# Moving the left-over scores, the left-over value products and one transposed block of x inside the head-pair loop

## The chip, the cores and the metric

The kernel runs on one core of one Trainium2 chip. The metric is the device time of one execution in microseconds (us). The core's engines are TensorE (PE, with its weight loads shown as PEld), VectorE (DVE), ScalarE (ACT), GpSimd (POOL) and SyncE (SP); each works through its own instructions in order, and semaphores tie them together.

## The reference, cut to what matters

Two layers follow one another: causal attention with a cumulative bias, and a mixing of 64 Fourier modes with a channel product behind it.

```
# q, k, v: (8, 8, 576, 64); s: (8, 8, 576)
scores = q @ k^T / 8;  bias = -(cumsum(max(s,0))[t] - cumsum(max(s,0))[t'])
attn   = softmax(causal(scores + min(bias, 0)))
x      = (attn @ v) with the heads side by side            # (8, 576, 512)
X      = rfft(x, axis=1)[:, :64]                           # 64 modes
Y      = X * (w_r + i w_i), one 512 x 512 matrix per mode  # 2 x 64 matrices from HBM
u      = x + irfft(Y)
out    = u + max(u @ w_ch, 0)
```

All that must be read once is q, k, v and the mode matrices; the latter, 64 x 2 of 512 x 512 in float32, are by far the most.

## The kernel before

**The loop.** N = 32 groups n = 0..31 each hold one pair of heads of one batch: `g, b = divmod(n, 8)`, with four head pairs g and eight batches b. For each group PE makes the scores of both heads (`scores`, h = 0 and 1, in two halves c = 0, 1 of the keys), ACT takes their exponentials into `p_sb`, and PE multiplies them with v (`av`), one group or half a group later. The 576 keys are two windows of 288; 128 + 128 of a window's keys go through the two halves c, and the 32 keys left over in each window go, for both heads together, through `scores4` (lines 368 to 391) into `p4`.

**Order within a group** (lines 586 to 621). This order is written by hand and is each engine's program order: `scores(n, 0)`, `av(n-1, 1)`, `mode_products(n)` where the group has any, `transposes(n+1, 0)`, `scores(n, 1)` with `scores4(n)` in front of its second half, `first_transposed(i, 0)`, `transposes(n+1, 1)`, `fft(n-1)`, `av(n, 0)`, on odd n `place_v(n+1)`, then `first_product(i, 0)`, `first_transposed(i, 1)`, `first_product(i, 1)`. The three steps with i exist in the last six groups (n = 26 to 31) alone: they multiply two token blocks of x, already finished, with w_ch ahead of time. Groups 8, 16 and 24 have another order (lines 595 to 603).

**What the steps do on the engines.** `transposes` (348) turns 18 blocks of q and k on PE into `tr_ps`; for half 0 DVE copies both q and k out (`qt`, `kt`), for half 1 DVE copies q and ACT copies k. `fft` (456) multiplies x of the last group with the Fourier matrix into `ft_ps`, and DVE casts it out in four pieces (line 474). `modes` (476) multiplies the modes with their weight tiles, 16 matmuls for one c of eight, in four steps of four that each need another weight tile; its sum goes to `y_acc` on DVE (502, 504), or for the last g to `y_sb` (508). `first_transposed` (550) makes four transposing matmuls into `xt_ps`, and DVE casts them to `xt1`. `first_product` (561) makes four matmuls into `z1_ps` (`z_ps` in the profile), and ACT copies the sum away (545).

**Accumulator memory.** The pools turn over buffers in the order in which they are asked for. `scpool` has two (scores, left-over scores, placed v), `trpool` one, `avpool` one, `auxpool` two (`yp`, `ft_ps`, `xt_ps`, `z1_ps`). Whoever asks takes the buffer asked for two requests ago (one in `trpool` and `avpool`), and waits until its readers are done.

**Loads.** POOL issues all large loads, in one fixed order (lines 243 to 272, 589): q and k for two groups, v for two groups, and 128 weight tiles of the modes (two transfers of 256 KB each as written), spread between them. A load waits for a free buffer (weights in rings of 11 and 6) and for its lane. SP issues the bias rows (346), small spreads of rows (519) and the stores.

**After the loop** (lines 864 to 967) come the modes of the last g, c = 0 to 7, with the remaining products of x and w_ch between them, and then the inverse transform, the ReLU, the sums and the stores, in a written order. The last weight tiles are used by c = 7 in line 899, whose fourth step follows `first_u`.

Of the kernel before, what the change touches and what calls it, by code (L numbers as in the profile page):

```python
# [18 lines left out]
def kernel(  # L19
# [15 lines left out]
    P = 128  # L35
# [7 lines left out]
    NCH = D + 1  # L43
# [89 lines left out]
    v4 = [ap_.tile([P, 2, 2, VW], FP16, name=f"v4_{i}") for i in range(2)]  # L133
# [6 lines left out]
    p4 = [ap_.tile([P, SP], FP16, name=f"p4_{i}") for i in range(2)]  # L140
# [207 lines left out]
    def transposes(n, half):  # L348
        if n >= N:
            return  # L350
        src = loaded[n][:, n % 2, :].rearrange("p (r d) -> p r d", d=D)[:, half * RH : half * RH + RH]
        ps = trpool.tile([P, RH, 2 * RP], BF16, name="tr_ps", tag="tr")
        for r in range(RH):
            for i in range(2):
                rows = slice(HP * i, HP * i + HP)
                nc.tensor.transpose(ps[rows, r, :], src[rows, r, :], ident16[rows, rows])  # L356
        for i, dst in enumerate((qt, kt)):
            copy = (nc.vector.tensor_copy, nc.scalar.copy)[half * i]
            to, rows = dst[n % NQ][:D], ps[HP * i : HP * i + HP]
            if i == 0:  # L360
                to = to.rearrange("d h (p r) -> d h p r", r=R)[:, :, :, half * RH : half * RH + RH]
                rows = rows.rearrange("d r (h p) -> d h p r", h=2)
            else:
                to = to.rearrange("d h (w r p x) -> d (h w) r p x", w=NWN, r=RV, x=2)[..., half]
                rows = rows.rearrange("d r (i p) -> d i r p", i=2 * NWN)
            copy(out=to, in_=rows)  # L366

    def scores4(n):

        g, b = divmod(n, B)  # L370
        ps = scpool.tile([P, 1024], FP32, name="sc_ps", tag="sc")
        cols = [ps[:, 512 * w : 512 * w + W] for w in range(NWN)]
        for w in range(NWN):
            nc.tensor.matmul(
                cols[w], ident16, negm[:, 2 * W + w * W : 2 * W + (w + 1) * W],
                start=True, stop=False, skip_group_check=True,
            )
        for wq_ in range(NWN):
            for wk in range(wq_ + 1):
                for h in range(2):  # L380
                    r0 = HP * h + RP * wk
                    nc.tensor.matmul(
                        cols[wq_][r0 : r0 + RP], kt[n % NQ][:, h, wk * W + 2 * P : (wk + 1) * W],
                        qt[n % NQ][:, h, wq_ * W : (wq_ + 1) * W],
                        start=False, stop=True, tile_position=(0, r0), skip_group_check=True,
                    )
        nc.scalar.activation(
            out=p4[n % 2][:, :S].rearrange("p (w t) -> p w t", w=NWN),
            in_=ps.rearrange("p (w t) -> p w t", w=NWN)[:, :, :W], func=ACTF.Exp,
            bias=cumt4[:, b * (H // 2) + g : b * (H // 2) + g + 1], scale=0.125,  # L390
        )

    def scores(n, h):
        g, b = divmod(n, B)
        pidx = b * H + 2 * g + h
        qh = qt[n % NQ][:, h, :]
        pt = p_sb[(2 * n + h) % NP_]
        for c in range(2):
            if h == 1 and c == 1:
                scores4(n)  # L400
            ps = scpool.tile([P, 1024], FP32, name="sc_ps", tag="sc")

            for w in range(NWN):
                nc.tensor.matmul(  # L404
                    ps[:, bass.ds(w * S, W)], ident16, negm[:, bass.ts(c, W)],
                    start=True, stop=False, skip_group_check=True,
                )
            for w, i0, i1 in ((0, 0, 512), (0, 512, S), (1, W, S)):
                c0 = w * S + i0 - w * W
                nc.tensor.matmul(  # L410
                    ps[:, c0 : c0 + i1 - i0], kt[n % NQ][:, h, bass.ds(w * W + c * P, P)], qh[:, i0:i1],
                    start=False, stop=True, skip_group_check=True,
                )
            for w in range(NWN):
                x = 2 * w + c
                nc.scalar.activation(  # L416
                    out=pt[:, poff[x] : poff[x] + S - w * W], in_=ps[:, w * S : (w + 1) * S - w * W],
                    func=ACTF.Exp, bias=cumt_sb[:, x, pidx : pidx + 1], scale=0.125,
                )
# [7 lines left out]
    def av(n, h):  # L427
        if n < 0:
            return
        g, b = divmod(n, B)  # L430
        pt = p_sb[(2 * n + h) % NP_]
        ps = avpool.tile([P, NT, VW], FP32, name="av_ps", tag="av")
        todo = []
        for I in range(NT):
            t0 = first_token(b, I)
            for x in range(2 * min((t0 + P - 1) // W + 1, NWN)):
                w, c = divmod(x, 2)
                o = poff[x] + t0 - w * W
                todo.append((I, pt[:, o : o + P], v2[n // 2 % 2][:, NWN * h + w, n % 2, c, :NCH]))
            todo.append((I, p4[n % 2][:, t0 : t0 + P], v4[n // 2 % 2][:, h, n % 2, :NCH]))  # L440

        for i, (I, lhsT, rhs) in enumerate(todo):
            nc.tensor.matmul(  # L443
                ps[:, I, :NCH], lhsT, rhs, start=(i == 0), stop=(i == len(todo) - 1),
                skip_group_check=True,
            )
        rcp = rpool.tile([P, NT], FP32, name="rcp", tag="rcp")
        nc.vector.reciprocal(out=rcp, in_=ps[:, :, D])  # L448
        nc.vector.tensor_tensor(  # L449
            out=x_all[:, g, b, :, D * h : D * h + D],  # L450
            in0=ps[:, :, :D],
            in1=rcp.unsqueeze(2).to_broadcast([P, NT, D]),
            op=ALU.mult,
        )
# [95 lines left out]
    def first_transposed(i, x):  # L550
        b, T = pairs[i][x]
        ps = auxpool.tile([P, DT, P], FP32, name="xt_ps", tag="aux")
        for dt in range(DT):
            nc.tensor.matmul(
                ps[:, dt, :], x_all[:, dt, b, T, :], ident16h, start=True, stop=True,
                skip_group_check=True,
            )
        xts1[i, x] = spool.tile([P, DT, P], FP16, name="xt1", tag="yt")
        nc.vector.tensor_copy(out=xts1[i, x], in_=ps)
# [13 lines left out]
    def mode_products(n, half=None):  # L573
        cs = mode_steps.get(n, [])
        for c in cs if half is None else cs[2 * half : 2 * half + 2]:
            modes(c // NCK, c % NCK)

    with tc.tile_pool(name="sc_psum", bufs=2, space=PSUM) as scpool, \
            tc.tile_pool(name="tr_psum", bufs=1, space=PSUM) as trpool, \
            tc.tile_pool(name="av_psum", bufs=1, space=PSUM) as avpool:  # L580
        cum_rows(0)
        transposes(0, 0)
        transposes(0, 1)
        load(loads_qk(2) + loads_v(2))
        pad_p()
        for n in range(N):
            if n in (0, 2):
                nc.vector.memset(xs_flat[n // 2].bitcast(FP32), 0.0)
            load(loads_qk(n + LA) + loads_v(n + LA) if n % 2 else [], loads_w(on_chip[n]))
            if n == N // 2 + 1:  # L590
                nc.gpsimd.dma_start(out=wch_sb, in_=moe_w_ch.rearrange("(dt p) e -> p dt e", p=P))
            cum_rows(n + 1)
            scores(n, 0)
            av(n - 1, 1)
            if n and n % B == 0:
                scores(n, 1)
                fft(n - 1)
                av(n, 0)
                mode_products(n, 0)
                transposes(n + 1, 0)  # L600
                mode_products(n, 1)
                transposes(n + 1, 1)
                continue
            mode_products(n)
            transposes(n + 1, 0)
            scores(n, 1)
            i = first_pairs[n - N + len(first_pairs)] if n >= N - len(first_pairs) else None
            if i is not None:
                first_transposed(i, 0)
            transposes(n + 1, 1)  # L610
            if n == 0:
                place_v(0)
            fft(n - 1)
            av(n, 0)
            if n % 2:
                place_v(n + 1)
            if i is not None:
                first_product(i, 0)
                first_transposed(i, 1)
            if i is not None:  # L620
                first_product(i, 1)
        av(N - 1, 1)
        fft(N - 1)
# [374 lines left out]
```

## Time and profile before

| | |
|---|---|
| median of 3 runs | 445.63 us (445.6 to 445.71) |
| profiled execution | 445.48 us, span of the profile 443.7 us |
| mean granted TensorE clock | 0.95 |
| PE busy | 351.0 us, 79% |
| ACT, DVE, POOL busy | 258.2, 249.7, 201.8 us |
| DMA | 93.64 MB moved, mean 211 GB/s over the span |

The page and the trace give times from the start of the span. The span leaves out 1.8 us of the execution around it. Busy shares are averages over stages: the loop ends at about 341 us, the modes of the last g run to about 407 us, and the rest finishes and stores the result. A row of a timeline has start, duration, engine, line, operation, output and inputs, count, and in brackets the idle time before it and what ended it. A row of the chain of waits has start, duration and what the time was spent on.

### The profile page before, as it was taken

What the parts mean: (1) busy time and instruction counts of PE and PEld (TensorE: products, weight loads), DVE (VectorE), ACT (ScalarE), POOL (GpSimd) and SP (SyncE); (2) the same over time, 40 slices, a digit from 0 to 9 for tenths busy, and PEclk for the clock granted to TensorE, in tenths of its full rate; (3) what the DMA queues carried; (4) which work ended last, traced back from release to release, by engine and by line L of the source; (5) the groups of instructions that cost most, each with busy time, mean ns of one, the idle gap of its engine ahead of it and who ended that gap; (6) DMA issues with size and microseconds to landing.
All of it is one profiled execution on the core that took longest, in us unless ns stands there. A gap on an engine that the chain in (4) does not pass through costs nothing.

```text
span 443.7 us, 12029 instructions
## 1 busy us (share of the span) xinstructions
PE 351.0 (79%) x5021; PEld 215.5 (49%) x5081; DVE 249.7 (56%) x539; ACT 258.2 (58%) x453; POOL 201.8 (45%) x326
## 2 busy tenths in 40 slices
PE   1578888888898877886957777888887997779992
PEld 1256565555665645654535344555553555433340
DVE  7747566456665654663543534555645554462893
ACT  1388888727877836774655355666662354320992
POOL 5454444443544444444444444444454444420591
PEclk9999999989999998999797988999999799998997
DMA  8999999999999999999999999999999999992696
GB/s 184 213 210 209 209 210 209 209 211 209 209 210 208 209 210 209 208 209 210 209 210 209 210 209 204 209 209 210 210 209 210 209 208 210 204 215 65 231 390 244
DMA packets 55510, 93.64 MB, mean 211 GB/s; under 512 B 8400, under 2 KB 14032, under 8 KB 55456
## 3 DMA queue, kind: packets, MB, share of 16 engines
q0 software_dynamic: 46144, 81.28, 98.9%
q1 hardware_dynamic: 9312, 11.58, 7.9%
q8 instruction: 40, 0.66, 0.5%
q14 instruction: 14, 0.11, 0.1%
HBM read 163.81 MB, written 9.44 MB: 390 GB/s over the span
## 4 chain that ended last, share of the span: by engine, by line
PE 53%; DMA 16%; ACT 14%; DVE 11%; issue 3%; DVEq 0%; ACTq 0%
DMA w_sb<-in_moe_w_r_dram 9%; ACT p_sb L416 9%; PE sc_ps L410 8%; PE sc_ps L404 7%; PE yp L484 6%; PE av_ps L443 6%; PE z_ps L679 5%; DMA w_sb<-in_moe_w_i_dram 4%; PE tr_ps L356 4%; PE ft_ps L464 2%; ACT v L197 2%; DMA qk<-in_k_dram 2%; ACT kt L366 2%; PE z_ps L567 2%; PE u_ps L805 2%
## 5 line engine op out<-in xcount | busy, mean ns | idle before, releaser
L416 ACT ACTIVATE p_sb<-sc_ps,cumt_sb 128x576 f16<-128x576 f32 (+1 forms) x256 | 142.0, 621 | 69.2 <-PE sc_ps L410 68.2
L247 POOL DMA_DIRECT2D w_sb<-in_moe_w_i_dram x120 | 71.0, 592 | 82.7 <-DMA w_sb<-in_moe_w_i_dram 29.5
L247 POOL DMA_DIRECT2D w_sb<-in_moe_w_r_dram x120 | 71.2, 594 | 78.0 <-DMA w_sb<-in_moe_w_r_dram 27.6
L404 PE MATMUL sc_ps<-negm,ident 128*128 128x288 bf16 x256 | 55.0, 298 | 25.2 <-ACT p_sb L416 19.2
L366 DVE COPY qt<-tr_ps 64x576 bf16<-64x576 bf16 x64 | 47.8, 746 | 47.3 <-PE tr_ps L356 47.3
L410 PE MATMUL sc_ps<-qt,kt 128*128 128x64 bf16 (+2 forms) x324 | 58.4, 281 | 10.2 <-ACT kt L366 5.8
L410 PEld LDWEIGHTS <-kt 128*128 128x128 bf16 x384 | 37.9, 101 | 34.2 <-ACT kt L366 10.5
L443 PE MATMUL av_ps<-v,p_sb 128*128 128x65 f16 x1024 | 51.7, 196 | 1.7 <-ACT v L197 1.7
L443 PEld LDWEIGHTS <-p_sb 128*128 128x128 f16 x1024 | 46.1, 98 | 6.3 <-issue 1.9
L443 PE MATMUL av_ps<-v,p 128*128 128x65 f16 x320 | 48.7, 194 | 0.0
L366 ACT COPY kt<-tr_ps 64x576 bf16<-64x576 bf16 x32 | 25.8, 805 | 39.1 <-DVE qt L366 38.5
L356 PE MATMUL tr_ps<-ident,qk 64*64 64x64 bf16 x1152 | 32.4, 201 | 19.5 <-DMA qk<-in_k_dram 9.2
L448 DVE RECIPROCAL rcp<-av_ps 128x5 f32<-128x5 f32 x64 | 12.4, 194 | 59.4 <-PE av_ps L443 58.4
L484 PE MATMUL yp<-w_sb,xs 128*32 128x512 bf16 (+1 forms) x480 | 39.9, 417 | 4.8 <-DMA w_sb<-in_moe_w_i_dram 3.3
L474 DVE CAST xs<-ft_ps 64x128 bf16<-64x128 f32 x128 | 36.7, 287 | 10.1 <-PE ft_ps L464 8.6
L356 PEld LDWEIGHTS <-qk 64*64 64x64 bf16 x1152 | 25.0, 114 | 32.9 <-DVE kt L366 9.7
L404 PEld LDWEIGHTS <-ident 128*128 128x128 bf16 x256 | 20.5, 98 | 41.6 <-issue 38.0
L449 DVE TENSOR_TENSOR x_all<-av_ps,rcp 128x320 f16<-128x320 f32 x64 | 31.5, 492 | 2.2
L443 PEld LDWEIGHTS <-p 128*128 128x128 f16 x320 | 31.6, 100 | 0.0
L484 PEld LDWEIGHTS <-xs 128*32 128x32 bf16 (+1 forms) x512 | 18.2, 145 | 21.2 <-issue 8.1
L366 DVE COPY kt<-tr_ps 64x576 bf16<-64x576 bf16 x32 | 25.6, 801 | 0.4
L545 ACT COPY z<-z_ps 128x512 f32<-128x512 f32 x22 | 12.9, 588 | 19.4 <-PE z_ps L567 11.2
(113 smaller groups left out, 495.0 us busy)
## 6 DMA issues: line engine op xcount, KB each, us to landing
w_sb<-in_moe_w_r_dram POOLq DMA_DIRECT2D x120, 256.0 KB, 9.9
w_sb<-in_moe_w_i_dram POOLq DMA_DIRECT2D x117, 256.0 KB, 9.9
out_dram<-r_w SPq DMA_DIRECT2D x16, 512.0 KB, 3.7
qk<-in_q_dram POOLq DMA_DIRECT2D x15, 288.0 KB, 9.6
qk<-in_k_dram POOLq DMA_DIRECT2D x15, 288.0 KB, 10.1
vf<-in_v_dram POOLq DMA_DIRECT2D x15, 288.0 KB, 10.1
x_all<-in_moe_w_i_dram POOLq DMA_DIRECT2D x6, 256.0 KB, 9.9
y_acc<-in_moe_w_r_dram POOLq DMA_DIRECT2D x4, 256.0 KB, 9.2
```

Of the source, the lines that this page charges most:

```text
L247: nc.gpsimd.dma_start(out=dst, in_=src)
L356: nc.tensor.transpose(ps[rows, r, :], src[rows, r, :], ident16[rows, rows])
L366: copy(out=to, in_=rows)
L404: nc.tensor.matmul(ps[:, bass.ds(w * S, W)], ident16, negm[:, bass.ts(c, W)], start=True, stop=False, skip_group_check=True,)
L410: nc.tensor.matmul(ps[:, c0 : c0 + i1 - i0], kt[n % NQ][:, h, bass.ds(w * W + c * P, P)], qh[:, i0:i1], start=False, stop=True, skip_group ...
L416: nc.scalar.activation(out=pt[:, poff[x] : poff[x] + S - w * W], in_=ps[:, w * S : (w + 1) * S - w * W], func=ACTF.Exp, bias=cumt_sb[:, x, ...
L443: nc.tensor.matmul(ps[:, I, :NCH], lhsT, rhs, start=(i == 0), stop=(i == len(todo) - 1), skip_group_check=True,)
L449: nc.vector.tensor_tensor(out=x_all[:, g, b, :, D * h : D * h + D], in0=ps[:, :, :D], in1=rcp.unsqueeze(2).to_broadcast([P, NT, D]), op=AL ...
L474: nc.vector.tensor_copy(out=xs[g % 2][HP * h : HP * h + HP, q_, :, h, :, b, :], in_=a)
L484: nc.tensor.matmul(ps[32 * cg : 32 * cg + 32, :], cols[k0:, q_, 1 - ri, :, c * MC // 2 + cg], wt[(g, c, ri, cg // 2)][k0:, 2 * (cg % 2) + ...
L545: nc.scalar.copy(out=z1s[i][:, xx], in_=z)
L679: nc.tensor.matmul(zs[i, x], xts[i][:, x, dt, :], wch_sb[:, dt, :], start=(dt == 0), stop=(last and dt == DT - 1), skip_group_check=True,)
```

## The change

Three moves of steps, none added or taken away. `scores4(n)` is called from the loop, between `mode_products(n)` and `transposes(n+1, 0)` (in groups 8, 16 and 24 in front of `scores(n, 1)`), and no more inside `scores(n, 1)`. `first_transposed(i, 1)` stands between `fft(n-1)` and `av(n, 0)`. In `av` the five products with the left-over keys `p4` come after all products with `p_sb`.

```
@@ scores
         for c in range(2):
-            if h == 1 and c == 1:
-                scores4(n)
             ps = scpool.tile([P, 1024], FP32, name="sc_ps", tag="sc")
@@ av
-        todo = []
+        todo, left = [], []
         for I in range(NT):
...
-            todo.append((I, p4[n % 2][:, t0 : t0 + P], v4[n // 2 % 2][:, h, n % 2, :NCH]))
-
+            left.append((I, p4[n % 2][:, t0 : t0 + P], v4[n // 2 % 2][:, h, n % 2, :NCH]))
+
+        todo = todo + left
@@ the loop
             if n and n % B == 0:
+                scores4(n)
                 scores(n, 1)
...
             mode_products(n)
+            scores4(n)
             transposes(n + 1, 0)
             scores(n, 1)
...
             fft(n - 1)
+            if i is not None:
+                first_transposed(i, 1)
             av(n, 0)
             if n % 2:
                 place_v(n + 1)
             if i is not None:
                 first_product(i, 0)
-                first_transposed(i, 1)
-            if i is not None:
                 first_product(i, 1)
```

More of the change, by code (lines that the diff above doesn't have):

```diff
@@ L398, in scores @@
         for c in range(2):
-            if h == 1 and c == 1:
-                scores4(n)
             ps = scpool.tile([P, 1024], FP32, name="sc_ps", tag="sc")
@@ L432, in av @@
         ps = avpool.tile([P, NT, VW], FP32, name="av_ps", tag="av")
-        todo = []
+        todo, left = [], []
         for I in range(NT):
@@ L439, in av @@
                 todo.append((I, pt[:, o : o + P], v2[n // 2 % 2][:, NWN * h + w, n % 2, c, :NCH]))
-            todo.append((I, p4[n % 2][:, t0 : t0 + P], v4[n // 2 % 2][:, h, n % 2, :NCH]))
+            left.append((I, p4[n % 2][:, t0 : t0 + P], v4[n // 2 % 2][:, h, n % 2, :NCH]))
+        todo = todo + left
         for i, (I, lhsT, rhs) in enumerate(todo):
@@ L595 @@
             if n and n % B == 0:
+                scores4(n)
                 scores(n, 1)
@@ L604 @@
             mode_products(n)
+            scores4(n)
             transposes(n + 1, 0)
@@ L613 @@
             fft(n - 1)
+            if i is not None:
+                first_transposed(i, 1)
             av(n, 0)
@@ L618 @@
                 first_product(i, 0)
-                first_transposed(i, 1)
-            if i is not None:
                 first_product(i, 1)
```

## The prediction

> **What bounds the kernel now.** I read the page's DMA row first, then the waits by stage, then the chain and the timeline around the last weights.
>
> ```profile
> DMA  8999999999999999999999999999999999992696
> ...
> q0 software_dynamic: 46144, 81.28, 98.9%
> ```
>
> The DMA engines are full from the start to slice 36 (396 us), at the 209 to 210 GB/s that the windows give. POOL's loads have one order and no spare rate: work done sooner does not make the stream end sooner. Where does the work wait for it? The waits from 200 to 273 us (who waits for whom: us in total, times, longest):
>
> ```profile
> PE tr_ps L356 <- DMA qk<-in_k_dram: 9.2, 2, 5.1
> PE yp L484 <- DMA w_sb<-in_moe_w_i_dram: 3.3, 2, 2.0
> ```
>
> And from 275 to 342 us, the last six groups:
>
> ```profile
> PE z_ps L567 <- DVE xt L559: 5.2, 6, 1.0
> ...
> PE sc_ps L404 <- ACT p_sb L416: 3.5, 6, 0.7
> ```
>
> In the first stretch PE waits for loads, in the second it waits for ACT and DVE alone. The chain changes its nature there:
>
> ```profile
> 262.89 10.00 DMA w_sb<-in_moe_w_i_dram
> 272.94 0.68 PE yp L484 x5
> ```
>
> A weight tile lands at 272.89 us, the middle of group 26 waits for it, and from there the chain is engine work only. So anything saved before 273 us is waited away, and what counts are groups 26 (its second half) to 31. PE has two stalls in each of them; group 28's:
>
> ```profile
> 298.53 0.74 ACT L387 ACTIVATE p<-sc_ps,cumt 128x576 f16<-128x576 f32 x1
> 298.69 0.41 PE L404 MATMUL sc_ps<-negm,ident 128*128 128x288 bf16 x2 [0.68 <-ACT p_sb L416]
> ...
> 303.58 1.04 PE L567 MATMUL z_ps<-wch_sb,xt 128*128 128x512 f16 x4 [0.95 <-DVE xt L559]
> ```
>
> The last half of the scores waits for the score buffer of head 1's first half, and the second product with w_ch waits for the DVE cast of the block just transposed. The end of the stream, by POOL's timeline, by the DMA view of that moment (its last column is us from issue to landing) and by the chain:
>
> ```profile
> 392.88 0.59 POOL L247 DMA_DIRECT2D w_sb<-in_moe_w_i_dram  x1 [0.61 <-DMA w_sb<-in_moe_w_i_dram]
> ```
> ```profile
> w_sb<-in_moe_w_i_dram POOLq DMA_DIRECT2D x1, 256.0 KB, 10.6
> ```
> ```profile
> 404.84 0.58 PE yp L484 x4
> ...
> 406.82 0.60 PE yp L484 x4
> ```
>
> The very last weight transfer is issued at 392.88 and takes 10.6 us, so it lands at 403.5. Its four matmuls run at 406.8. PE is late for it by 406.8 - 403.5 = 3.3 us. That is all that a faster loop can win.
>
> **The change part by part.** Counts of instructions stay; only places change. No load and no store is moved; on POOL's and SP's queues nothing is passed.
>
> *Left-over scores.* Score buffers turn A, B. Before: head 0 A, B; head 1's first half A; left-over B; last half A, which waits for exponentials that have just begun. After: A, B, left-over A, head 1 B, A. The last half now waits for the left-over exponential. In group 28's times (from the group's start at 293.24) the products before it end at 2.98, left-over scores take 0.76 (297.25 to 298.01), to 3.74; ACT has been free since 3.03 and its 0.74 end near 4.6; the transposes (0.40) and head 1's first half (0.63) bring PE to 4.77. So the 0.68 goes. In group 31, without transposes, about 0.25 stays.
>
> What is queued behind the moved step is `transposes(n+1, 0)`, 0.76 later, and DVE's copies of it: 0.74 + 0.80 from 4.22 to 5.77 us. `trpool` has one buffer, so the second transposes must wait for 5.77; PE is there at 5.70. Cost 0.1 us, hidden by the first transposed block of x (0.32). Groups before 26 lack that cover and would pay about 0.45 of the 0.68; the DMA waits above (9.2 + 3.3 us) hide either sign.
>
> *Second transposed block.* The block (0.35) is made at 6.87 instead of after the first product; its DVE cast of 0.69 lies beside `av` (0.65) and the first product (0.92). The 0.79 to 0.95 stall goes. But `auxpool` turns over in a new order: the first product now takes the buffer of `ft_ps` and waits for its four casts. DVE's string in program order, from 4.22: q and k copies to 5.77; cast of the first block to 6.5; q copy to 7.2; four casts (1.18) to 8.3 to 8.45. PE arrives at 7.87 in even groups, at 8.42 in odd ones, which place v (0.55) in between. New wait: 0.5 to 0.6 even, 0 to 0.1 odd. The second product follows at 9.4, its cast done at about 9.1: no wait. A group ends near 10.25 us; group 28 took 11.2 and 29 took 11.7.
>
> Delayed on DVE by the moved cast is the normalisation of `av(n, 0)`, by 0.7 us to 9.9; its next readers are the next group's `av` (buffer) and `fft`, over 1 us later. Free.
>
> *Left-over products last* in `av`: the same 21 matmuls. It helps only if `p4` is late; with the exponential at 4.6 us and `av(n, 0)` at 7.2, it is not. Zero.
>
> *Sum of the loop.* Group 26 (slow clock in its middle hides one stall already) 0.4, group 27 (no mode products) 1.25, 28: 0.95, 29: 1.4, 30: 0.95, 31: 0.85, together 5.8 us; gross 5.2 + 3.5 = 8.7, less 2.9 of new waits. Bounds: 8.7 if DVE's string overlaps better; -3.5 if the copies of one `tr_ps` bank come one by one into PE's path (the slow rival). I take 5.8, worked from this stage's own rows.
>
> *From 341 us on.* All moves forward 5.8 us until weights are late. Working landings out from issue plus time to landing, as above: c = 5's last tile lands at 382.4, used at 386.84 + 0.55, so 5.0 us may be won; c = 6's at 392.6 (issued about 384.3, landing near 8), used at 396.4, so 3.8; c = 7's, 3.3. Between c = 6 and c = 7 PE needs casts, transposes and products (3.7 us at full clock), ready for c = 7's third tile (400.7) and again for its fourth (403.5). Hence the last matmuls start near 403.5. SP's row spreads of c = 6 (two of 128 KB) now fall into the full stream: 0 to 0.6 us on the last landing; I take 0.2. What lies behind 407 us is untouched and shifts as a block.
>
> Sum against the profiled execution: 445.48 - 3.3 + 0.2 = 442.4. It lies 0.15 below the median of 445.63, so the forecast is 442.5.
>
> *The clock, row against rule.* Two windows and the two after them:
>
> ```profile
> 338.30:341.71 3.41, 1.61 (x22) 0.83 (x19) 2.21 (x7) 0.06 (x1) 1.18 (x2) 1.00 1.12 210
> 341.71:345.12 3.41, 3.18 (x16) 1.31 (x17) 1.50 (x4) 0.00 (x0) 2.12 (x4) 0.50 1.12 211
> ...
> 382.67:386.08 3.41, 1.85 (x23) 0.90 (x23) 0.69 (x1) 1.18 (x2) 2.36 (x4) 1.00 1.11 199
> 386.08:389.49 3.41, 2.96 (x33) 1.45 (x32) 2.26 (x4) 0.33 (x1) 1.54 (x4) 1.00 1.10 203
> ```
>
> After 3.41 us with PE busy 1.61 the granted clock was 0.50; after 1.85 it stayed 1.00. My walk puts 1.9 to 2.3 us of work into each such stretch from 389.5 to 403 us, where PE will wait for weights: close. One halved stretch costs at most 1.7 us, and only behind 403.5; in front of it the weights cover it. The Trainium skill ("TensorE: Matmul & The Clock Gate", "What's actually happening") says that the clock halves after an idle window of about 3.4 us. By that rule my waits of 1 us could never halve it, and the sum would stay; by the rows, half idle is enough, and I keep up to 1.7 us in the range.
>
> **The rivals.**
> - *Part of it*: DVE's string ends later than I have it, or a halved clock falls behind the last weights, and 1 to 2.5 us are left: 443.0 to 444.6. For it: the close margins above. Against: 5.8 is won where 3.3 is needed.
> - *Hidden*: the last weights land some 3 us later because the freed work draws small transfers into the full stream, or the loop wins under 0.9 us: 444.8 to 446.4, 445.6 in the middle. Against: 3 us are 0.6 MB at 210 GB/s, and the spreads are 0.26 MB.
> - *Slower*: DVE becomes the bound of the last six groups. Place: the first product's wait for the casts of `ft_ps`. My string has 0.97 us to spare a group (5.8 / 6); ending later by d costs d a group, so from d = 1.1 the total is worse by over 0.9 us. One more exposed pair of copies (0.74 + 0.80 = 1.54) gives 6 x (1.54 - 0.97) = +3.4, so 449.0. For it: ACT's k copy waits for DVE's q copy already. Against: DVE is busy 5.83 of 11 us at 275 to 286.
> - *It does nothing*: true of the third move alone.
>
> **How the numbers follow.** Forecast case (441.8 to 443.0) 0.70, part 0.16, hidden 0.07, slower 0.07. The range runs from 441.4 (the stream ends 1 us sooner) to 444.6, which takes in the part case and leaves out both others. A measurement of this kernel tells 0.2% (0.9 us) from no change: faster 0.86, same 0.07, slower 0.07.
>
> **What would show it.** The waits of line 404 for line 416 fall from 0.7 to about 0 in the last six groups, those of line 567 for line 559 vanish, and a new one of line 567 for line 474 of about 0.5 us stands in even groups; the first modes of the last g start near 335 instead of 340.9; PE waits for `w_sb` at c = 5, 6 and 7; the last weights land at 403 to 404 and the last `yp` runs right after. I am wrong if the last landing moves by over 1 us, if the six groups stay at 11 us, or if the time between the last `yp` and the end is not the same 37 us.

## The result and the profile after

The changed kernel is faster: 443.44 us median against 445.52 us of the kernel before beside it, ratio of the mean times 0.9962 with a 95% interval of 0.9947 to 0.9978, so 1 to 2.4 us, 1.7 us in the middle. Forecast were 442.5 us and 3.1 us less. The profiled execution took 444.91 us (span 443.1), the longest of the changed kernel's 17 (443.04 to 444.91), so its span alone understates the gain. (Two later profiles of the kernel before came from disturbed executions, with spans of 792 and 475 us; nothing is read from them.)

The page of after shows the same full stream, ending at the same slice:

```profile
DMA  8999999999999999999999999999999999994696
...
q0 software_dynamic: 46144, 81.28, 99.2%
```

PE's waits from 275 to 342 us, the last six groups:

```profile
PE vp_ps L192 <- DMA vf<-in_v_dram: 1.6, 1, 1.6
PE z_ps L566 <- DVE xs L473: 1.2, 3, 0.4
```

Both old stalls (5.2 and 3.5 us) are gone. In their place stand the forecast wait for the casts of `ft_ps` (lines have moved by one: 566 and 473 are 567 and 474 of before), 0.4 us in each of three even groups, and a wait for v's load that was not forecast. Then the first modes of the last g, by the timeline:

```profile
335.70 1.06 PE L483 MATMUL yp<-w_sb,xs 128*32 128x512 bf16 x8 [0.98 <-DVE xs L473]
```

They began at 340.90 before, by the chain:

```profile
340.90 3.08 PE yp L484 x13
```

So 5.2 us are won at the end of the loop. Now the end of the weight stream, by POOL's last issue, the DMA view of that moment and the chain:

```profile
394.42 0.59 POOL L247 DMA_DIRECT2D w_sb<-in_moe_w_i_dram  x1 [0.43 <-DMA w_sb<-in_moe_w_i_dram]
```
```profile
w_sb<-in_moe_w_i_dram POOLq DMA_DIRECT2D x1, 256.0 KB, 11.3
```
```profile
399.60 1.07 PE yp L483 x2
...
404.28 0.58 PE yp L483 x4
406.26 0.60 PE yp L483 x4
```

The last weights are issued at 394.42 and land at 405.7, 2.2 us later than in the trace of before (392.88 + 10.6 = 403.5). The four matmuls that use them start at 406.19 by the timeline (406.26 in the chain). Before, they started at 406.75:

```profile
406.75 0.65 PE L484 MATMUL yp<-w_sb,xs 128*32 128x512 bf16 x4
```

That is only 0.6 us sooner. Of 5.2 us won, this execution keeps 0.6. Why the stream ended later is what the experiments are about.

### The profile page after: what moved, and what is told of

It is laid out like the page before. It is cut to its first block, busy times and chain, and to the rows that moved or that the text cites. A ratio compares the mean times of both kernels' runs of the same rounds, so it can differ in the third digit from the quotient of the medians.

```text
span 443.1 us, 12104 instructions
## 1 busy us (share of the span) xinstructions
PE 360.0 (81%) x5081; PEld 215.0 (49%) x5081; DVE 252.3 (57%) x539; ACT 257.2 (58%) x453; POOL 201.8 (46%) x326
## 4 chain that ended last, share of the span: by engine, by line
DMA 63%; PE 21%; DVE 7%; issue 4%; ACT 3%; POOL 0%; DVEq 0%; POOLq 0%; ACTq 0%
DMA w_sb<-in_moe_w_r_dram 30%; DMA w_sb<-in_moe_w_i_dram 11%; DMA vf<-in_v_dram 9%; DMA qk<-in_q_dram 9%; DMA qt<-ncum_sb 3%; PE av_ps L442 2%; PE sc_ps L408 2%; DMA qk<-in_k_dram 2%; DVE qt L366 2%; PE z_ps L776 2%; PE u_ps L806 2%; PE z_ps L566 2%; PE yp L483 2%; PE u_ps L776 2%; PE tr_ps L356 2%
## 5 line engine op out<-in xcount | busy, mean ns | idle before, releaser
L414 ACT ACTIVATE p_sb<-sc_ps,cumt_sb 128x576 f16<-128x576 f32 (+1 forms) x256 | 138.7, 622 | 40.4 <-PE sc_ps L408 39.3
L408 PE MATMUL sc_ps<-qt,kt 128*128 128x512 bf16 (+2 forms) x384 | 72.7, 301 | 7.0 <-ACT kt L366 4.4
L483 PE MATMUL yp<-w_sb,xs 128*32 128x512 bf16 (+1 forms) x480 | 43.5, 430 | 7.5 <-DMA w_sb<-in_moe_w_i_dram 5.7
L366 ACT COPY kt<-tr_ps 64x576 bf16<-64x576 bf16 x32 | 25.7, 804 | 37.2 <-DVE qt L366 36.4
L442 PE MATMUL av_ps<-v,p_sb 128*128 128x65 f16 x1024 | 44.2, 196 | 1.7 <-ACT v L197 1.7
L442 PEld LDWEIGHTS <-p_sb 128*128 128x128 f16 x1024 | 38.9, 99 | 5.9 <-issue 2.3
L387 ACT ACTIVATE p<-sc_ps,cumt 128x576 f16<-128x576 f32 x32 | 23.8, 745 | 26.7 <-PE sc_ps L382 26.1
L463 PE MATMUL ft_ps<-Ff_sb,x_all 128*64 128x192 f16 (+1 forms) x320 | 24.0, 262 | 0.8 <-DVE x_all L448 0.8
L680 PE MATMUL z_ps<-wch_sb,xs 128*128 128x512 f16 x96 | 23.3, 387 | 0.2 <-DVE xs L671 0.2
## 6 DMA issues: line engine op xcount, KB each, us to landing
qk<-in_k_dram POOLq DMA_DIRECT2D x15, 288.0 KB, 10.1
```

Of the source, the lines that this page charges most:

```text
L387: nc.scalar.activation(out=p4[n % 2][:, :S].rearrange("p (w t) -> p w t", w=NWN), in_=ps.rearrange("p (w t) -> p w t", w=NWN)[:, :, :W], f ...
L408: nc.tensor.matmul(ps[:, c0 : c0 + i1 - i0], kt[n % NQ][:, h, bass.ds(w * W + c * P, P)], qh[:, i0:i1], start=False, stop=True, skip_group ...
L414: nc.scalar.activation(out=pt[:, poff[x] : poff[x] + S - w * W], in_=ps[:, w * S : (w + 1) * S - w * W], func=ACTF.Exp, bias=cumt_sb[:, x, ...
L442: nc.tensor.matmul(ps[:, I, :NCH], lhsT, rhs, start=(i == 0), stop=(i == len(todo) - 1), skip_group_check=True,)
L463: nc.tensor.matmul(ps[HP * q_ : HP * q_ + HP].rearrange("p h f -> p (h f)"), x_all[:nT, g, b, T, q_::2], Ff_sb[:nT, T, :], start=(T == 0), ...
L483: nc.tensor.matmul(ps[32 * cg : 32 * cg + 32, :], cols[k0:, q_, 1 - ri, :, c * MC // 2 + cg], wt[(g, c, ri, cg // 2)][k0:, 2 * (cg % 2) + ...
```

## Experiments

Two numbers of each trace are compared below: the *gate*, the landing of the last tile of group 26's modes, from which the work of before is no more held by loads (272.9 us in the first trace), and the *last landing*, that of the last weights. Both are issue plus time to landing, as above. The *last start* is that of the last four matmuls with weights, from the timeline.

**The kernel before once more.** The kernel unchanged, in three further runs.

> The kernel before once more, for a second trace of the end of the weight stream. Theory 'stream' (the last weight tile bounds the changed kernel, and when it lands differs from execution to execution by a us or more): the last weights land anywhere from 402.5 to 405.5 us and not at 403.4 again. Theory 'engines' (the stream is as steady as the time of this kernel in its first runs, and the changed kernel is held by PE's slow clock alone): they land at 403.2 to 403.7. Time the same as before, ratio 1.000 within 0.003 in both.

> The kernel before, for the second trace that the first attempt did not give in an undisturbed execution. The four traces with moved steps have the last weights landing at 404.5 to 406.2 us, the one trace of before at 403.4. Theory 'the stream moves from execution to execution': they land at 404 to 406 here too, with the last matmuls with weights still near 406.8 or later. Theory 'the moved steps push the stream': 403.2 to 403.7 again. In both the time from the start of the last four matmuls with weights to the end of the span is 37.0 us, as in all five traces. Ratio 1.000.

The first two gave times only: ratios 0.9991 (0.9967 to 1.0016) and 0.9998 (0.9979 to 1.0017) to the runs of before beside them.

> The kernel before, for a trace at full clock; the first two more traces came from executions at 792 and 475 us. Theory 'the stream moves from execution to execution': the last tile of group 26's modes lands between 272.7 and 274.3 and the last weights at 403.4 to 405.0, with the distance of 21.1 us between the last tiles of c = 5 and c = 7 kept, because its spreads of c = 6 come later than in the changed kernel. The last matmuls with weights start near 406.8, up to 1 us later where the stream is late. Theory 'the moved steps push the stream': all as in the first trace, 272.9 and 403.4.

Ratio 0.9999 (0.998 to 1.0018). Gate 273.03, last landing 403.85, last start 406.96, by the chain:

```profile
405.05 0.58 PE yp L484 x4
407.03 0.60 PE yp L484 x4
```

This trace agrees with both theories on the stream: its gate and its last landing are 0.1 and 0.4 us off those of the first trace. The kernel of before with a shortened stream (below), whose order of work up to group 26 is the same, has its gate at 273.96, and the transposed block alone, also with the old order up to there, at 274.12. So one order of work gives gates 1.2 us apart: that part of the lateness is not made by the change.

**The changed kernel once more.**

> The changed kernel once more, for a second trace. Theory 'stream': the first modes of the last g start near 335.7 us again, the last weights land between 403.5 and 406, and the last matmuls with weights start within 1 us of that landing. Theory 'engines': last weights land at 405.7 again as the changed order of work pushes them, and the last matmuls with weights start over 1 us later wherever the clock is halved at 397 to 404. Ratio to before 0.996 in both.

Ratio 0.997 (0.9951 to 0.999). Gate 272.95, last landing 404.54, and the last start by the timeline:

```profile
402.05 0.65 PE L483 MATMUL yp<-w_sb,xs 128*32 128x512 bf16 x4 [0.56 <-DMA w_sb<-in_moe_w_i_dram]
...
404.58 0.65 PE L483 MATMUL yp<-w_sb,xs 128*32 128x512 bf16 x4 [0.47 <-DMA w_sb<-in_moe_w_i_dram]
```

The last two groups of matmuls both wait for their weights, and the last starts 0.04 us after the landing. The first modes of the last g start at 334.05, 1.65 us sooner than in the first trace of the changed kernel; the gate lies 1.2 us sooner. The execution took 443.4 us with a span of 441.6. Here the stream bounds.

**The moves by themselves.** First the left-over scores, with the left-over products last; the transposed block put back:

```
             fft(n - 1)
-            if i is not None:
-                first_transposed(i, 1)
             av(n, 0)
...
                 first_product(i, 0)
+                first_transposed(i, 1)
```

> The changed kernel with the second transposed block put back behind the first product; the left-over scores stay moved. The loop should win about 3 us (groups 26 to 31: 0.2, 0.5 and four times 0.4 to 0.7), so the first modes of the last g start near 338. Theory 'stream' (only what is needed up to the last weights' landing is kept, some 2 us): nearly the whole gain stays, ratio 0.995 to 0.998. Theory 'adds up' (each part wins its own stalls and the sum is the gain): about half of it, ratio 0.997 to 0.999.

Ratio 0.9981 (0.9962 to 1.0). Gate 273.72; the first modes of the last g start at 338.26; last landing 405.64, and

```profile
405.68 0.65 PE L483 MATMUL yp<-w_sb,xs 128*32 128x512 bf16 x4 [0.26 <-DMA w_sb<-in_moe_w_i_dram]
```

Then the kernel before with the opposite edit:

```
             fft(n - 1)
+            if i is not None:
+                first_transposed(i, 1)
             av(n, 0)
...
-                first_transposed(i, 1)
```

> The kernel before with only the second transposed block moved in front of the value products. The 0.8 to 0.95 us stall goes, the wait of the first product for the four casts comes instead in even groups (about 0.5), the 0.68 us stall in the scores stays; the loop wins about 3 us, first modes of the last g near 338. Theory 'stream': ratio 0.995 to 0.998, and the gains of this and of the left-over scores alone sum to more than the gain of both together. Theory 'adds up': 0.997 to 0.999, and they sum to the whole.

Ratio 0.9985 (0.9964 to 1.0005). Gate 274.12; first modes at 337.51; last landing 406.16, last start 407.15.

From the gate to the first modes of the last g it is 68.0 us before (340.90 - 272.89; 68.1 in the second trace), 64.5 with the scores alone, 63.4 with the block alone, 61.5 and 61.1 with both. Taken alone the moves win 3.5 and 4.6 us, together 8.1, but both in one kernel win only 6.5 to 6.9. TensorE's clock bears on the difference. A row of the windows has the stretch, its length, the busy us of PE, PEld, DVE, ACT and POOL with their instruction counts, the granted clock, the DMA share and GB/s. Just behind the gate the clock was halved in all three traces without a move (the two of before, and before with the short stream below) and full in all traces with a moved step. Before and the block alone:

```profile
273.45:276.86 3.41, 3.21 (x34) 1.61 (x33) 2.18 (x3) 1.22 (x3) 1.50 (x3) 0.50 1.12 207
274.16:277.57 3.41, 2.72 (x39) 1.60 (x41) 2.15 (x3) 1.52 (x3) 1.78 (x3) 1.00 1.10 205
```

The block alone has the old order of work up to `fft(25)` in group 26, and yet this step starts 4.4 us after the gate there, 5.3 before. So 0.8 to 0.9 us of its win is this clock. If the clock is worth as much in the other kernels, adding the two wins counts it twice; and the wait for v, 0.8 us with the scores alone and nothing with the block alone, is 1.6 and 1.2 with both. What keeps the clock up there, the moves or the place of the gate, is not shown. In the time nothing can be told from these ratios: their intervals lie over one another. Nor do the traces rank the two moves. The scores alone start the last matmuls at the landing; the block alone, which won more in the loop, starts them 1 us late, but there the clock was halved from 398.8 to 405.6:

```profile
402.23:405.64 3.41, 3.41 (x14) 0.73 (x12) 0.00 (x0) 0.00 (x0) 0.00 (x0) 0.50 0.38 77
```

And the third move undone on the changed kernel:

```
-            left.append((I, p4[n % 2][:, t0 : t0 + P], v4[n // 2 % 2][:, h, n % 2, :NCH]))
+            todo.append((I, p4[n % 2][:, t0 : t0 + P], v4[n // 2 % 2][:, h, n % 2, :NCH]))
```

> The changed kernel with the left-over value products back in their old places. Prediction: the third move alone does nothing, since the left-over exponentials are ready over 2 us before the value products; loop and ratio as in the changed kernel, first modes of the last g at 334 to 336, ratio 0.995 to 0.998. Rival: the products in their old places wait for the exponentials in the early groups; then the loop is later by a visible amount and ratio is 0.998 or more.

Ratio 0.9966 (0.9953 to 0.998). Gate 272.90, first modes at 334.19, 61.3 us later, as with it. The third move does nothing that can be seen.

**A shorter stream.** In both kernels two weight tiles of the last g are not loaded:

```
             g, c, ri, par = key = wq[len(wt)]
+            if (g, c, par) == (NG - 1, 1, 1):
+                wt[key] = wt[g, c, ri, 0]
+                continue
```

> The changed kernel without the loads of two weight tiles (four transfers, 5.0 us of the stream): the modes c = 1 of the last g use the first tile for both halves. Theory 'stream': the last weights land about 5 us sooner, near 400, and the time falls until the engines bound, whose last matmuls with weights would start at 406.8 - 5.2 = 401.6 without any wait: 3 us below the changed kernel, near 440.5, ratio 0.988 to 0.991. Theory 'engines': the time stays, ratio 0.996.

> The kernel before without the loads of the same two weight tiles (the modes c = 1 of the last g use the first tile for both halves). Theory 'stream': before the change PE is late for the last weights, so a stream that ends 5 us sooner gives next to nothing, ratio 0.997 to 1.000. Theory 'the stream bounds before and after alike': it falls as much as the changed kernel does, ratio 0.99.

The changed kernel: 438.62 us, ratio 0.9847 (0.9822 to 0.9872), 6.8 us under before. The kernel before: ratio 0.9978 (0.9955 to 1.0002). The same four transfers are worth about 5 us behind the change, more than was expected, and 0 to 2 us ahead of it. In the shortened kernel of before POOL waits 8.0 us for PE's `yp`, its stream is paced by PE, and its last weights land at 402.52, 128.6 us after its gate (130.55 in the first trace of before); its last matmuls start 133.8 us after the gate, as without the edit. In the shortened changed kernel the last landing is 398.6 and the chain is PE's:

```profile
398.16 0.54 PE u_ps L809 x2
398.69 0.43 PE u_ps L779 x2
399.13 0.43 PE u_ps L790 x2
399.56 0.60 PE yp L486 x4
```

No weight is waited for there any more: the engines alone can start the last matmuls 126.7 us after the gate (399.49 - 272.78). The changed kernel with its whole stream needs 131.5 to 132.4 (the versions with the third move undone and with the filler below among them), the kernel before 133.9 (406.75 - 272.89; 406.96 - 273.03; 133.8 = 407.80 - 273.96 with the short stream). The engines won 7 us; the stream lets through about 2. I had put the engine bound 2 us too late. The 133.9 us are engine time with a slow stretch in it; before, shortly ahead of the last matmuls:

```profile
399.74:403.15 3.41, 3.41 (x14) 0.87 (x15) 0.69 (x1) 0.00 (x0) 0.00 (x0) 0.50 0.55 116
```

All three traces without a move have such a stretch there. How much of the 3.3 us by which PE was late a full clock there would have won without the moves, no run tells.

**The spreads of c = 6.** Two times 128 KB that SP sends into the stream are put behind the last weights, on POOL's queue:

```
-        nc.sync.dma_start(out=yv[16 * c : 16 * c + 16, :, which, :], in_=rows)
+        queue = nc.gpsimd if c == NCK - 2 else nc.sync
+        queue.dma_start(out=yv[16 * c : 16 * c + 16, :, which, :], in_=rows)
```

> The changed kernel with the two spreads of c = 6's rows (128 KB each) issued on POOL's queue, behind the last weights, in place of SP's. In the trace of before the last tile of c = 7 lands 21.1 us after the last tile of c = 5, in the traces with moved steps 21.5 to 22.1. Theory 'the spreads take 0.9 us of the stream': it is 21.1 again, and the time falls by 0.5 to 0.9 us below the changed kernel's, ratio to before 0.994 to 0.996. Theory 'they do not matter': 22 us, and the time stays.

442.93 us, ratio 0.9956 (0.9941 to 0.9972). The last tile of c = 5 lands at 382.75, the last weights at 403.67: 20.9 us, where the changed kernel has 22.0 and 22.1 and the kernel before 21.1 and 21.3. The time is 0.5 us below the changed kernel's median in the first comparison, and the intervals of the two ratios lie over one another. The last matmuls start at the landing:

```profile
403.71 0.65 PE L483 MATMUL yp<-w_sb,xs 128*32 128x512 bf16 x4
```

**The clock.** PE is kept at work in two waits:

```
+    def filler(k):
+        ps = auxpool.tile([P, DM], FP32, name="fill_ps", tag="aux")
+        for _ in range(k):
+            nc.tensor.matmul(ps, ident16h, wch_sb[:, 0, :], start=True, stop=True, skip_group_check=True)
     yb6 = modes(NG - 1, c)
+    filler(3)
     yt = y_transposed(yb6)
+    filler(3)
     vb6 = y_times_wch(c, yt)
```

> The changed kernel with twice three idle matmuls of 512 columns, whose result nobody reads, in PE's two waits between the modes c = 6 and the product with w_ch behind them. Theory 'weights first' (the halved clock near 397 to 404 lies in front of the last weights and is covered): the clock stays at 1.00 there and the time changes by less than 0.5 us, ratio to before 0.995 to 0.998. Theory 'clock': the changed kernel loses over 1 us to it, ratio 0.993 to 0.995.

Ratio 0.9983 (0.9969 to 0.9997): no gain, and a little above the range of the first theory. The windows of this kernel show the clock up where the trace of after had 0.50:

```profile
396.00:399.40 3.40, 2.43 (x15) 0.71 (x11) 0.69 (x1) 0.59 (x1) 0.00 (x0) 1.00 1.13 210
399.40:402.80 3.40, 2.61 (x16) 0.87 (x16) 0.00 (x0) 0.00 (x0) 0.00 (x0) 1.00 0.96 172
```

And the time PE gains it waits away:

```profile
403.25 0.65 PE L483 MATMUL yp<-w_sb,xs 128*32 128x512 bf16 x4 [0.88 <-DMA w_sb<-in_moe_w_i_dram]
...
405.90 0.65 PE L483 MATMUL yp<-w_sb,xs 128*32 128x512 bf16 x4 [0.59 <-DMA w_sb<-in_moe_w_i_dram]
```

The last landing is 405.85. The clock is not what holds this kernel; in the trace of after it can have cost at most the 0.5 us between landing and last start.

> Both of the last two edits together on the changed kernel. Theory 'weights first': as the moved spreads alone, ratio 0.994 to 0.996, the last matmuls with weights within 0.3 us of the last landing. Theory 'clock': both add, ratio 0.991 to 0.993.

443.35 us, ratio 0.996 (0.9945 to 0.9975). Gate 274.32, last landing 405.81, last start 405.85; from c = 5's last tile to the last weights 21.5 us. That is between the two values of the spreads' theory; by this distance the spreads take 0.5 to 1.2 us (22.0 and 22.1 against 21.5 and 20.9). Counted from the gate it is less sure: the last weights land 130.7 and 131.5 us after it with the spreads behind, 131.4 to 132.3 without the edit, so one of the two traces shows a gain and the other next to none. In the time it is not told apart: the version with the spreads behind the weights has the lowest median of all that load everything, but its interval covers the changed kernel's ratio.

**All traces together.** Times in us:

```
kernel              gate    last landing  last start   span    last start - gate
before              272.89  403.44        406.75       443.7   133.9
before, third       273.03  403.85        406.96       443.9   133.9
changed             274.19  405.68        406.19       443.1   132.0
changed again       272.95  404.54        404.58       441.6   131.6
left undone         272.90  405.21        405.26       442.2   132.4
scores alone        273.72  405.64        405.68       442.7   132.0
block alone         274.12  406.16        407.15       444.1   133.0
filled              274.45  405.85        405.90       442.9   131.5
spreads behind      272.94  403.67        403.71       440.9   130.8
filled and spreads  274.32  405.81        405.85       443.0   131.5
```

From the last start to the end of the span it is 36.9 to 37.2 us in all ten. The time is thus the last start plus a block of 37 us. Before, that start is set by the engines, 133.9 us after the gate in both traces; after, by the last landing, at which the last matmuls start at once in six of the eight traces with moved steps. The two others, changed and block alone, are 0.5 and 1.0 us later and have the clock halved for 6.83 us in front of the last start.

## Why the prediction was right, and where its size was off

The direction, the bound and the range held; the gain was a third to three quarters of the forecast 3.1 us (1.0 to 2.4). The term that was mis-sized is the landing of the last weights behind the change: 0.2 us later was forecast, and it came 0.6 to 1.8 us later.

*Before 273 us nothing counts*: right. In the early groups the last half of the scores no longer waits (13.4 us in all from 14 to 200 us before), and the second transposes wait for DVE's copies instead. The same stretch of after:

```profile
PE tr_ps L356 <- DVE kt L366: 13.9, 21, 5.5
```

It was 7.0 us in 2 waits; 19 more waits take 6.9 us, 0.36 each where 0.45 was forecast. The gate hides all of that.

*The loop*: the stalls right, the sum near by luck in part. The score stall went to nothing in the last six groups, the product's stall became 0.4 us in the even ones (0.5 to 0.6 forecast) and nothing in the odd ones; from modes to modes groups take 10.1 us (304.82 to 314.97: 10.15; forecast 10.25). Forecast were 5.8 us; 5.2 in the profiled pair, and 6.5 to 6.9 counted from the gate. Two things that the sum did not expect work against each other. The clock behind the gate, taken as slow in group 26, was full (some 0.9 us won, as above). `place_v` in group 27 waits for v's load: 1.6 and 1.2 us in the two traces of the changed kernel, 0.8 to 1.4 in the others with moved scores, with early and late gates alike, and nothing before. So groups 26 and 27 won 1.7 and 2.1 us from gate to modes, near the 1.65 forecast, because the two nearly cancel; groups 28 to 31 won 4.8 where 4.15 were forecast.

*The end*: right that the last weights set it and that the change can keep no more than PE was late for them. That lateness was 3.3 and 3.1 us in the two traces of before. PE waits for weights at c = 5, 6 and 7 as forecast (0.2, 1.0 and 0.5 us in the trace of after), and behind the last `yp` stand the same 37 us. The term that failed is the landing behind the change: "0 to 0.6 us on the last landing; I take 0.2". The last weights land 131.4 to 132.3 us after the gate in the traces with both moves and SP's spreads, against 130.55 and 130.8 before: 0.6 to 1.8 us later. By its own sign, a last landing moved by over 1 us, the prediction was wrong here. The spreads may be a part of it: the two of c = 6 are issued 3.0 and 3.5 us sooner, at 395.59 and 398.82, though the first of them lay in front of the last weights before too (398.59). From the gate to the last landing SP's queue moves 0.58 MB where it moved 0.45 and 0.51, which is 0.3 to 0.6 us at 210 GB/s; putting the spreads behind gave back 0.5 to 1.2 us by the distance from c = 5, in one of two traces by that from the gate. What the rest is, is open. Nor was it quite so that work done sooner can't help the stream: before, POOL's issue at 383.72 had waited 3.0 us for PE's `yp`, a wait that the trace of after has not got; and still the stream of after ended later.

So 133.9 - 131.9, 2.0 us, is to be had on the mean of the four traces with both moves and SP's spreads (changed twice, left undone, filled: 132.0, 131.6, 132.4, 131.5), close to the 1.7 us (1.0 to 2.4) of the times. Left over beside it is the stream's own place: the gate moves between 272.8 and 274.5 us from execution to execution, and takes both kernels with it, since before is paced from the gate too. A landing read from one trace was good to about 1.5 us, and the forecast used it to 0.1.

*The clock*: it was halved from 397.27 to 404.09 in the trace of after, in line with the rows' measure (PE busy 1.61 of 3.41 us in front of it) and not with that of an idle window:

```profile
393.85:397.26 3.41, 1.61 (x13) 0.74 (x14) 1.19 (x2) 0.58 (x1) 0.73 (x2) 1.00 1.12 223
397.27:400.68 3.41, 2.88 (x12) 0.47 (x10) 0.69 (x1) 0.00 (x0) 0.00 (x0) 0.50 1.11 221
```

The Trainium skill's page "TensorE: Matmul & The Clock Gate" ("What's actually happening") has the clock fall after an idle window; here, as in the trace of before, a window a little under half busy was enough. It lay in front of the last weights, and the last start was 0.5 us behind the landing in that execution; the filled kernel shows that with the clock up the time is no better. The same had happened before at 399.74 to 403.15, which the prediction's rows left out, so some of the 3.3 us of lateness, by an estimate at most 1.7 (half of that stretch), was slow clock.

*The rivals.* The median of 443.44 us lies in the interval of "part of it" (443.0 to 444.6, given 0.16) and not in that of the forecast case (441.8 to 443.0, given 0.70). The cause was neither of the two named there, DVE and the clock behind the last weights. It is the one named under "hidden", last weights that land later, at 0.6 to 1.8 us in place of some 3. "Slower" did not come: DVE's string ended where it was put. "It does nothing" holds for the third move, as said.

## What to carry to other kernels

When transfers fill the machine to a late point, find the last load and the moment of its use: the distance is all that faster work can win, whatever the stalls removed are worth (here 7 us of engine time became about 2). Read that landing from several executions, and count what the faster work itself will send into the stream before the last load, since small stores that used to come behind it can now come in front. A second kernel with a shortened stream tells at once which side sets the time.

## What was not expected of the hardware

The same order of loads, at the same 209 to 210 GB/s, reached one and the same tile at 272.8 to 274.5 us in the twelve traces that the experiments rest on: six lie between 272.8 and 273.0, six between 273.7 and 274.5. In the pair of traces of before and after the difference is there early: the first half of the tenth weight tile lands at 44.4 and 46.0. That is no rule, since the block alone has 44.4 there and 274.1 later. And the last transfer took 10.2 to 11.3 us to land in eleven of the twelve traces (12.1 in the kernel of before with the short stream), where the median of the weight loads is 9.9 us.
